# Cutting one V load of a decode attention kernel by partitions, with two small changes at head and tail

## The chip, the cores and the metric

The kernel runs on one core of a Trainium2 chip; the other cores are idle. The metric is the device time of the kernel in microseconds (us), as the median over runs. The kernel before takes 1254.60 us (1254.50 to 1254.62 in five runs), so differences of a few tenths of a us can be seen.

## The reference

One query token attends to 4,096 keys and values, for 8 x 32 = 256 heads of 128 elements, all in bf16:

```
q: (8, 32, 1, 128)   k, v: (8, 32, 4096, 128)
scores = einsum('bhqd,bhkd->bhqk', q, k) * 128 ** -0.5
attn   = softmax(scores)
out    = einsum('bhqk,bhkd->bhqd', attn, v)
```

K and V are 268 MB each and every byte is used once. The kernel is a stream of loads with some arithmetic beside it.

## The kernel before

The 256 heads are worked on in 32 tiles (NT) of 8 heads. A tile of K or of V is `[128 partitions, C = 256 positions, 128]` in bf16: 8 MB, one contiguous row of 64 KB for each partition. There are two K buffers and one V buffer. All loads are issued by SyncE, in program order; `cuts` says which loads are cut by position, and `("v", NT - 1)` is the last load of all.

```python
    cuts = {
        ("k", 0): [C // 4, C // 4, C // 2],
        ("k", NT - 4): [C // 2] * 2,
        # ... NT - 3, NT - 2, NT - 1 are cut as well
        ("v", NT - 1): [C // 2, C // 4, C // 8, C // 16, C // 32, LAST, LAST],
    }

    def load(kind, t):
        # ... choose pool and buffer
        c0 = 0
        for n in cuts.get((kind, t), [C]):
            nc.sync.dma_start(buf[:, c0 : c0 + n, :], src[t, :, c0 : c0 + n, :])
            c0 += n
            if kind == "k" and t == 0 and c0 == n:
                nc.sync.dma_start(q_all[:], q_n)
```

For each tile VectorE multiplies K by q and adds the two halves (in four quarters), TensorE sums the rest over the head dimension by matmuls with the identity, ScalarE makes the weights, and 64 matmuls apply them to V. At the end the sums are copied out of PSUM and combined:

```python
    def copy_of(t):
        comb = small.tile([P, CB, D], BF16, name="comb", tag="comb")
        av = avs.pop(t)[:].rearrange("p (m d) -> p m d", d=D)
        n = CB if t < NT - 1 else CB // 2
        nc.scalar.activation(out=comb[:, 0:n, :], in_=av[:, 0:n, :], func=ACT.Copy)
        if n < CB:
            nc.vector.tensor_copy(out=comb[:, n:CB, :], in_=av[:, n:CB, :])
        combs[t] = comb
```

## Time and profile before

| | before |
|---|---|
| median time | 1254.60 us |
| read from memory | 536.94 MB, 429 GB/s over the span |
| DMA engines busy | 99.3% (loads alone) |
| VectorE, TensorE, ScalarE busy | 77%, 44%, 27% |
| last landing mark of the last V load | 1248.64 us of a span of 1252.8 us |

The kernel is bound by its loads. The only idle DMA time is at the very end, where sixteen engines that begin level (the marks of the first load, explained below, lie within 0.4 us) do not end together. The lines of the page, the windows and the timeline that show this stand in the prediction below.

One view needs an explanation, because the argument rests on it. Every load of this kernel leaves sixteen *landing marks* in the trace. I read them as one for each DMA engine that took part: in 1,177 of the 1,252.8 us exactly sixteen packets of loads are under way (my count from the trace). The marks of one load, as a distance from its last one, show how far each engine is ahead. For the last load of the kernel before (my extract of the trace, us ahead of the last mark):

```
6.21 6.11 5.93 5.90 5.80 5.30 | 1.85 1.66 1.65 1.64 1.62 1.55 1.49 1.43 1.11 | 0
```

Six engines are early, nine are late, one is last. "Row" below means one packet of the trace, on one engine: 64 KB of a whole load (2.42 us in the median of 7,424), 32 KB of a half (1.22 us in the median of 1,152).

### The profile page before, as it was taken

The page shows a single profiled execution, that of the slowest core. Times are in us where ns is not written, and L with a number is a line of the kernel's source. Part 1 is how long each engine was busy: PE and PEld are TensorE (multiplying, and loading weights), DVE is VectorE, ACT ScalarE, POOL GpSimd, SP SyncE. Part 2 cuts the span into 40 slices and gives each one's busy share as a digit, 9 for nine tenths or more (in the row PEclk, how much of TensorE's full clock was granted, in tenths as well). Part 3 has the DMA queues.
Part 4 walks back from the last instruction along what each step waited for, and adds up shares of the span by engine and source line. Part 5 has one row for each costly group of instructions (what it writes and reads, how often), then busy time and mean ns, then how long its engine had stood idle before and what let it go on. Part 6 is the DMA issues. An engine that isn't in the chain of part 4 may idle for free.

```text
span 1252.8 us, 8134 instructions
## 1 busy us (share of the span) xinstructions
PE 554.0 (44%) x3299; PEld 202.6 (16%) x3299; DVE 967.6 (77%) x531; ACT 343.3 (27%) x625; POOL 6.0 (0%) x26
## 2 busy tenths in 40 slices
PE   2444543345534355333453334542445434545356
PEld 0111111111111111111111111111112111211112
DVE  7877887777977779777797777886778877977981
ACT  0333123331233321333213333123330333311333
POOL 1000000000000000000000000000000000000000
PEclk8667666667657767576765776666676766676777
DMA  9999999999999999999999999999999999999997
GB/s 404 435 436 432 434 435 433 434 432 434 435 434 436 434 429 429 431 432 433 434 434 436 430 436 436 436 434 435 432 427 427 437 433 432 434 420 431 430 439 311
DMA packets 11734, 537.53 MB, mean 429 GB/s; under 512 B 1840, under 2 KB 2096, under 8 KB 2352
## 3 DMA queue, kind: packets, MB, share of 16 engines
q1 hardware_dynamic: 11360, 536.94, 99.3%
q8 instruction: 26, 0.43, 0.1%
q10 hardware_dynamic: 336, 0.07, 0.0%
q14 instruction: 12, 0.10, 0.0%
HBM read 536.94 MB, written 0.07 MB: 429 GB/s over the span
## 4 chain that ended last, share of the span: by engine, by line
DMA 79%; PE 14%; DVE 6%; issue 0%; SPq 0%; another core or an unknown queue 0%; ACT 0%
DMA vt<-in_v_dram 78%; PE av L256 13%; DVE kt L175 3%; DVE kt L178 2%; PE ps L190 1%; DMA q_all<-in_q_dram 1%; DVE sc L202 0%; SPq L147 0%; DVE pmax L212 0%; DVE spread L214 0%; DVE nmax L219 0%; DVE comb L286 0%; ACT comb L284 0%; ACT stage L310 0%
## 5 line engine op out<-in xcount | busy, mean ns | idle before, releaser
L175 DVE TENSOR_TENSOR kt<-kt,qb 128x8192 bf16<-128x8192 bf16 x128 | 565.2, 4415 | 181.9 <-DMA kt<-in_k_dram 175.3
L190 PE MATMUL ps<-kt,ident 128*128 128x512 bf16 x1024 | 353.6, 508 | 572.1 <-DVE kt L178 572.1
L231 ACT ACTIVATE w<-sc,bias 128x256 bf16<-128x256 f32 x256 | 300.5, 1587 | 260.5 <-DVE bias L223 260.5
L178 DVE TENSOR_TENSOR kt<-kt 128x4096 bf16<-128x4096 bf16 x128 | 293.4, 2292 | 4.4
L190 PEld LDWEIGHTS <-ident 128*128 128x128 bf16 x1024 | 119.6, 119 | 775.5 <-issue 506.1
L256 PE MATMUL av<-vt,w 128*32 128x512 bf16 x2047 | 176.5, 513 | 90.0 <-DMA vt<-in_v_dram 90.0
L202 DVE TENSOR_REDUCE sc<-ps 128x64 f32<-128x512 f32 x128 | 87.8, 686 | 68.1 <-PE ps L190 68.1
L284 ACT ACTIVATE comb<-av 128x512 bf16<-128x512 f32 (+1 forms) x32 | 19.5, 609 | 413.1 <-PE av L256 413.1
L231 ACT ACTIVATION_READ_ACCUMULATOR w<-sc,bias 128x1 f32 x256 | 126.6, 495 | 0.0
L256 PEld LDWEIGHTS <-w 128*32 128x32 bf16 x2047 | 68.7, 125 | 207.1 <-DMA vt<-in_v_dram 107.8
L163 ACT ACTIVATE qg<-qh 8x128 bf16<-8x128 f32 x32 | 8.5, 266 | 165.9 <-PE qh L159 165.9
L310 ACT ACTIVATE stage<-op,rz 16x128 bf16<-16x128 f32 x16 | 5.9, 371 | 56.4 <-DVE rz L276 41.3
L301 PE MATMUL op<-comb,pick 128*16 128x128 bf16 x128 | 13.4, 230 | 12.8 <-ACT comb L284 12.4
L212 DVE TENSOR_REDUCE pmax<-sc 128x1 f32<-128x256 f32 x32 | 13.4, 420 | 1.1
L165 PE MATMUL qp<-qg,heads 8*128 8x128 bf16 x32 | 7.5, 235 | 12.7 <-ACT qg L163 12.7
L276 DVE RECIPROCAL rz<-zp 16x1 f32<-16x1 f32 x16 | 2.4, 149 | 13.9 <-PE zp L268 13.9
L159 PE MATMUL qh<-q_all,ident 128*8 128x128 bf16 x32 | 8.2, 256 | 8.3 <-DMA q_all<-in_q_dram 8.3
L167 ACT ACTIVATE qb<-qp 128x128 bf16<-128x128 f32 x32 | 8.9, 277 | 10.4 <-PE qp L165 10.4
L301 PEld LDWEIGHTS <-pick 128*16 128x16 bf16 x128 | 7.6, 91 | 21.0 <-issue 20.9
L214 DVE TENSOR_SCALAR spread<-same,pmax 128x32 f32<-128x32 f32 x32 | 7.7, 241 | 1.1
L223 DVE TENSOR_SCALAR bias<-own,nmax 128x8 f32<-128x8 f32 x32 | 7.4, 231 | 1.1
L219 DVE TRANSPOSE_TENSOR_REDUCE nmax<-spread 128x1 f32<-128x32 f32 x32 | 6.8, 211 | 1.1
(27 smaller groups left out, 20.1 us busy)
## 6 DMA issues: line engine op xcount, KB each, us to landing
kt<-in_k_dram SPq DMA_DIRECT2D x8, 4096.0 KB, 43.0
kt<-in_k_dram SPq DMA_DIRECT2D x4, 2048.0 KB, 23.3
vt<-in_v_dram SPq DMA_DIRECT2D x1, 4096.0 KB, 41.4
vt<-in_v_dram SPq DMA_DIRECT2D x1, 2048.0 KB, 45.9
vt<-in_v_dram SPq DMA_DIRECT2D x1, 1024.0 KB, 47.8
vt<-in_v_dram SPq DMA_DIRECT2D x1, 512.0 KB, 48.6
vt<-in_v_dram SPq DMA_DIRECT2D x31, 33.3
kt<-in_k_dram SPq DMA_DIRECT2D x27, 47.4
```

What stands on the lines that cost most here:

```text
L159: nc.tensor.matmul(qh[:], lhsT=ident[:, p0 : p0 + G], rhs=q_all[:, x, :], start=True, stop=True)
L163: nc.scalar.activation(out=qg[:], in_=qh[:], func=ACT.Copy)
L167: nc.scalar.activation(out=qb[:, 0, :], in_=qp[:], func=ACT.Copy)
L175: nc.vector.tensor_tensor(out=part, in0=part, in1=qb[:].to_broadcast([P, MC, D]), op=ALU.mult)
L178: nc.vector.tensor_tensor(out=part[:, :, 0 : D // 2], in0=part[:, :, 0 : D // 2], in1=part[:, :, D // 2 : D], op=ALU.add,)
L190: nc.tensor.matmul(ps[:], lhsT=ident[:], rhs=kt[:, u * UC : (u + 1) * UC, s * DS : (s + 1) * DS], start=(s == 0), stop=(s == n - 1),)
L202: nc.vector.tensor_reduce(out=scs[t][:, u * UC : (u + 1) * UC], in_=sums.pop((t, u))[:], axis=AX.X, op=ALU.add)
L212: nc.vector.tensor_reduce(out=pmax[:], in_=sc[:], axis=AX.X, op=ALU.max)
L231: nc.scalar.activation(out=w[:, :, g], in_=sc[:], func=ACT.Exp, bias=bias[:, g : g + 1], scale=scale, accum_out=esum[:, t % R, g : g + 1],)
L256: nc.tensor.matmul(avs[t][j * AG : (j + 1) * AG, :], lhsT=w[:, c0 : c0 + CB, :], rhs=vt[:, c0 : c0 + CB, :], start=(i < TG), stop=(j not i ...
L284: nc.scalar.activation(out=comb[:, 0:n, :], in_=av[:, 0:n, :], func=ACT.Copy)
L301: nc.tensor.matmul(ops[n][:], lhsT=pick[:, m, r, :], rhs=comb[:, m, :], start=(r == 0 and m == 0), stop=(r == R - 1 and m == CB - 1),)
```

## The change

Its intent can be read from the arithmetic. In one V load in the middle of the kernel, twelve engines carry one row less and four carry three more, which would even out the end. Beside that it starts with a longer first K piece, drops the cut of one late K load, puts three of the last tile's matmuls into other groups of sums, and makes the last copy in one piece.

```diff
-        ("k", 0): [C // 4, C // 4, C // 2],
-        ("k", NT - 4): [C // 2] * 2,
+        ("k", 0): [C // 2] * 2,
...
+        ("v", NT // 2): [C // 2] * 2,
...
-            nc.sync.dma_start(buf[:, c0 : c0 + n, :], src[t, :, c0 : c0 + n, :])
+            parts = [(0, P)]
+            if (kind, t, c0) == ("v", NT // 2, 0):
+                parts = [(0, P - 16)] + [(p, p + 4) for p in range(P - 16, P, 4)]
+            for lo, hi in parts:
+                nc.sync.dma_start(buf[lo:hi, c0 : c0 + n, :], src[t, lo:hi, c0 : c0 + n, :])
...
-            0 if t == NT - 1 and C // 2 <= c0 < 3 * C // 4 else c0 // CB % TG
+            0 if t == NT - 1 and C // 2 <= c0 < C // 2 + 3 * C // 16 else c0 // CB % TG
...
-        n = CB if t < NT - 1 else CB // 2
-        nc.scalar.activation(out=comb[:, 0:n, :], in_=av[:, 0:n, :], func=ACT.Copy)
-        if n < CB:
-            nc.vector.tensor_copy(out=comb[:, n:CB, :], in_=av[:, n:CB, :])
+        nc.scalar.activation(out=comb[:], in_=av, func=ACT.Copy)
```

## The prediction

> **What bounds the kernel now.** I read the page first: the slices over time, the DMA queues, the chain that ended last. Then I read the windows of the last 20 us, the chain and timeline of the tail, and the landing marks of single loads.
>
> ```profile
> DMA  9999999999999999999999999999999999999997
> GB/s 404 435 436 432 434 435 433 434 432 434 435 434 436 434 429 429 431 432 433 434 434 436 430 436 436 436 434 435 432 427 427 437 433 432 434 420 431 430 439 311
> ...
> q1 hardware_dynamic: 11360, 536.94, 99.3%
> q8 instruction: 26, 0.43, 0.1%
> ...
> q14 instruction: 12, 0.10, 0.0%
> ...
> DMA 79%; PE 14%; DVE 6%; issue 0%; SPq 0%; another core or an unknown queue 0%; ACT 0%
> ```
>
> The DMA row is 9 in every slice but the last, so transfers bound this kernel. VectorE (77% busy) and TensorE (44%) work in their shadow. The bytes, 536.94 MB, are fixed by the inputs. The change alters no byte, so it can win only at the head, at the tail, or in how evenly the sixteen DMA engines end. The windows of the tail show that last one (columns: stretch, length, busy time per engine, granted clock, DMA share, GB/s):
>
> ```profile
> 1230.00:1240.00 10.00, 4.95 (x64) 2.32 (x60) 0.00 (x0) 8.51 (x17) 0.21 (x1) 0.84 0.96 406
> 1240.00:1246.00 6.00, 4.69 (x37) 2.30 (x30) 0.15 (x1) 0.00 (x0) 0.00 (x0) 0.82 0.75 306
> 1246.00:1249.00 3.00, 2.94 (x26) 1.24 (x24) 0.00 (x0) 0.23 (x1) 0.00 (x0) 1.00 0.20 68
> ```
>
> The DMA share falls to 0.75 and then 0.20 while V is still arriving: some engines have finished and wait for the others. The landing marks give the amounts. Every load leaves sixteen, one per engine. For the last load they lie 6.2, 6.1, 5.9, 5.9, 5.8, 5.3 us (six engines), then 1.85 to 1.1 us (nine engines) before the last one, which alone sets 1248.64. The mean lead is 3.1 us: all that perfect balance could win. The lead grows steadily. The first load's marks lie within 0.4 us; at the V load with index 16, landing near 683.8 us, the six lead by 2.9 to 3.3 us.
>
> The cause can be read from the packets. A 64 KB row takes 2.42 us on its engine, back to back. The 26 instruction packets of 16 KB each hit one engine: beside one, a row took about 2.89 us and the next began about 1.07 us later, so a fetch costs its engine some 1.55 us. They come round about every 390 us, to eight different engines in turn. 26 x 1.55 = 40 us, plus the twelve 8 KB fetches at about 0.7 us (a stretched row and a 0.31 us gap), is 48.7 us; the sum of the sixteen leads is 49.2. So the skew is fetch time, and it falls on ten engines while six stay free.
>
> After the DMA ends, this remains (timeline):
>
> ```profile
> 1248.68 0.38 PE L296 MATMUL op<-vt,w_last 128*16 128x128 bf16 x4
> 1248.77 0.38 ACT L284 ACTIVATE comb<-av 128x256 bf16<-128x256 f32 x1 [10.26 <-PE av L256]
> 1249.19 0.42 DVE L286 CAST comb<-av 128x256 bf16<-128x256 f32 x1 [6.60 <-ACT comb L284]
> 1249.21 0.27 PE L301 MATMUL op<-comb,pick 128*16 128x128 bf16 x2
> 1249.67 0.27 PE L301 MATMUL op<-comb,pick 128*16 128x128 bf16 x2 [0.19 <-DVE comb L286]
> 1249.97 0.36 ACT L310 ACTIVATE stage<-op,rz 16x128 bf16<-16x128 f32 x1 [0.82 <-PE op L301]
> ```
>
> The two half copies do not run side by side: VectorE's waits for ScalarE's.
>
> [...]
>
> **The change part by part.**
> 1. The V load with index 16 comes in halves. In the first half, every engine carries 7 rows instead of 8[...]. A 32 KB row takes 1.21 us in the trace (1213 to 1221 ns). So twelve engines gain 1.21 us, and four lose 3 x 1.21 = 3.63 us. If the four are among the six free ones, they fall back by 4.84 us against the rest, from a lead of 5.3 to 6.2 us to one of 0.5 to 1.4 us. The last mark is then still one of the twelve's, 1.21 us earlier. At index 16 itself the lead is about 3 us, so that load lands 0.6 us later at most: 3.63 less 3. Its successor K load (19.3 us of transfer) hides that. **-1.2 us.** The size of the shift, 4.84 us, fits the lead so well that I take it for chosen after seeing which engines are ahead.
> 2. First K load: halves for quarters. The first quarter landed at 8.1 us; a half lands some 4.9 us later (2 MB at 430 GB/s). VectorE's first tile, done near 41 us, ends near 46, and K load 2 is issued then instead of at 40.98. V load 0 keeps the engines occupied until 61.6 us, so nothing runs dry. VectorE needs about 30 us of each 38.7 us period and catches up. **0.**
> 3. K load NT-4 whole: VectorE starts that tile 9.7 us later, but it has about 8 us of slack per tile, and the next three K loads are still cut. **0.**[...]
> 4. Group of the last tile's matmuls: the same 31 matmuls after the half, and each piece is awaited from DMA. **0.**
> 5. Last copy whole: removed are 0.38 + 0.42 us plus the handover, 1248.77 to 1249.61, 0.84 us. Added is one 128x512 ScalarE copy, mean 0.617 us. But two of the four result matmuls ran beside the VectorE half, and now all four follow; four took 0.39 to 0.59 us elsewhere, against 0.27. 0.84 - 0.62 - 0.12 = 0.1. **-0.1 us.**
> 6. Five more load instructions on SyncE at 0.33 to 0.46 us each; SyncE idles for hundreds of us. **0.**
>
> Sum: 1254.57 - 1.2 - 0.1 = 1253.3.
>
> **The rivals.**
> [...]
> - *Wrong engines.* If engines 0 to 3 are among the fetching ten, they set the end: between 1.11 us behind which they start and the last one itself, 3.63 us more is +1.8 to +3.6, near 1257. Nothing in the trace numbers its engines, so I can't exclude this.
> - *Hidden anyway.* If TensorE paced the tail, a DMA that ends 1.2 us earlier would win less. The weights are done at 1238.1, the 32 matmuls on the first half at 1242.35, and the next piece lands at 1243.65: 1.3 us of slack, just enough. 1254.
>
> **Range and chances.** I give 1253.3 by the sum about 60%, a partial or no gain (1253.7 to 1254.6) 15%, wrong engines 10%[...]. I predict 1253.4, a little above the sum; range 1252.3 to 1259[...]. Two per cent is 25 us: no case wins that[...].
>
> **What the profile after would show.** Right: in the last load's landing marks the spread shrinks from 6.2 to about 2 us, the DMA share of the last windows stays higher, and the last V mark comes near 1247.4. The tail holds one ScalarE copy of about 0.6 us, then four result matmuls. The VectorE start at 14 instead of 9.6 us leaves no trace later.[...] Wrong engines: rows of 1.21 us, but a spread above 6 us at the end.[...]

Its sum came to 1253.3 us (1254.57 - 1.2 - 0.1). Part 1 rests on the deal of rows above; before the run it was an assumption. "Engines 0 to 3", here and in the expectations, is only a name for the four engines that a 4-partition load uses: the trace doesn't number engines. Cut are what no trace or run of this case shows, and one rival with its 15%: that the four rows of a small load hold each other up. Its 1267 to 1272 us rested on an estimate, four rows of 1.21 us one after the other, 4.84 us for each small load. That the 16 KB fetches hit eight engines in turn is read from the packets: the rows just behind them take 2.88 to 2.97 us, and their lengths recur with every eighth fetch, 388.6 us later (65.75, 454.31, 842.87 us).

## The result, and the profile after

The changed kernel takes 1273.37 us (1272.88 to 1275.88, five runs) against 1254.60. The ratio is 1.0154 (95% interval 1.014 to 1.0168). Ratios here are the mean time of one kernel's fast runs over that of the other's fast runs of the same rounds, so not quite the ratio of the medians that I quote. The loss is 18.8 us: within two per cent, but far outside the stated range, and on the wrong side.

The page of the changed kernel, the same rows as shown of before:

```profile
DMA  9999999999999999999999999999999999999996
GB/s 406 454 427 428 427 433 431 429 444 431 429 430 429 444 429 436 433 431 431 429 385 277 439 431 431 430 437 431 438 434 429 428 431 438 436 433 419 431 439 264
...
DMA 82%; PE 14%; DVE 3%; another core or an unknown queue 0%; issue 0%; SPq 0%; ACT 0%
```

The DMA row is as full as before, but the engines moved less in the same time: 385 and 277 GB/s in the two slices from about 636 to 699 us, where V load 16 runs. **Busy is not moving at full speed**, and only the GB/s row tells. Windows of ten us make it sharp. First the kernel before (columns as in the prediction; the last is GB/s):

```profile
660.00:670.00 10.00, 0.00 (x0) 0.10 (x1) 5.51 (x2) 7.05 (x14) 0.00 (x0) 0.50 0.97 419
670.00:680.00 10.00, 6.04 (x17) 2.05 (x17) 9.97 (x6) 0.90 (x3) 0.00 (x0) 0.67 0.98 421
680.00:690.00 10.00, 6.84 (x66) 2.31 (x64) 9.97 (x4) 0.00 (x0) 0.00 (x0) 0.54 1.06 460
```

Then the changed kernel:

```profile
650.00:660.00 10.00, 4.27 (x26) 1.74 (x22) 6.25 (x8) 2.70 (x6) 0.00 (x0) 0.91 1.00 428
660.00:670.00 10.00, 0.00 (x0) 0.10 (x1) 1.97 (x1) 7.25 (x14) 0.00 (x0) 0.50 1.00 226
670.00:680.00 10.00, 3.98 (x10) 1.26 (x10) 9.93 (x5) 0.90 (x3) 0.00 (x0) 0.57 1.03 251
680.00:690.00 10.00, 3.13 (x8) 0.89 (x7) 9.97 (x6) 0.00 (x0) 0.00 (x0) 0.77 0.98 201
690.00:700.00 10.00, 3.60 (x32) 1.39 (x33) 5.98 (x2) 0.00 (x0) 0.00 (x0) 0.50 1.03 416
```

For 30 us the rate is about half (226 GB/s on average against 433). That alone is 30 x (1 - 226/433) = 14.3 us of lost transfer. In the packets of the trace, the 32 KB rows of the 112-partition load took 2.3 to 2.5 us in the main (2.36 in the median of the first 112), on *all sixteen* engines, in place of 1.21 (of the 23 rows that began between 664 and 668 us, none took less than 2.3), the last 64 KB rows of the K load before it up to 5.0 in place of 2.42, and rows of the full second half beside the small loads took 2.4 to 2.9.

In the chain of waits of the changed kernel, V load 16 is seen as a wait of 42.67 us and a second one, in place of about 33 us for the V loads before it and 35.02 for the next (start, length, what; the unknown queue is the second half, which landed at 703.75):

```profile
651.67 42.67 DMA vt<-in_v_dram
694.55 3.60 PE av L261 x32
698.15 5.60 another core or an unknown queue
703.80 3.63 PE av L261 x32
707.44 35.02 DMA vt<-in_v_dram
```

The end differs too. The windows of its last us:

```profile
1250.00:1260.00 10.00, 5.53 (x67) 2.86 (x63) 0.00 (x0) 7.63 (x15) 0.21 (x1) 0.67 0.88 365
1260.00:1264.00 4.00, 3.20 (x25) 1.40 (x18) 0.16 (x1) 0.00 (x0) 0.00 (x0) 0.71 0.20 81
1264.00:1268.00 4.00, 3.35 (x29) 1.39 (x28) 0.00 (x0) 0.42 (x1) 0.00 (x0) 1.00 0.09 34
```

A DMA share of 0.125 would be two engines of sixteen. From about 1262 us no more than that are at work. The landing marks of the last load say the same (us ahead of the last, at 1267.45):

```
11.24 10.88 10.60 9.84 | 7.05 6.99 6.96 6.95 6.68 6.60 6.53 6.23 5.90 5.28 | 1.17 0
```

The early group of six has become four, the late group ten, and two engines end more than 5 us after everybody else. So there are two losses. The engine that was last before is not one of the two (the probe below shows it), so at the slowest it now has the mark at 5.28: 1262.17 against 1248.64, **13.5 us** later; this is what the slow stretch costs all. The two stragglers add **5.3 us**. The sum is 18.8.

The tail after the loads went as foreseen (timeline of the changed kernel):

```profile
1267.49 0.38 PE L298 MATMUL op<-vt,w_last 128*16 128x128 bf16 x4
1267.58 0.60 ACT L288 ACTIVATE comb<-av 128x512 bf16<-128x512 f32 x1 [9.95 <-PE av L261]
1268.23 0.38 PE L303 MATMUL op<-comb,pick 128*16 128x128 bf16 x4 [0.36 <-ACT comb L288]
1268.65 0.36 ACT L312 ACTIVATE stage<-op,rz 16x128 bf16<-16x128 f32 x1 [0.47 <-PE op L303]
```

From the start of the copy to the start of the stage write it takes 1.07 us, against 1.20 before.

### The profile page after: what moved, and what is told of

It is laid out like the page before. It is cut to its first block, busy times and chain, and to the rows that moved or that the text cites. A ratio compares the mean times of both kernels' runs of the same rounds, so it can differ in the third digit from the quotient of the medians.

```text
span 1271.3 us, 8138 instructions
## 1 busy us (share of the span) xinstructions
PE 550.3 (43%) x3299; PEld 201.1 (16%) x3299; DVE 967.4 (76%) x530; ACT 343.3 (27%) x625; POOL 6.0 (0%) x26
## 4 chain that ended last, share of the span: by engine, by line
DMA 82%; PE 14%; DVE 3%; another core or an unknown queue 0%; issue 0%; SPq 0%; ACT 0%
DMA vt<-in_v_dram 78%; PE av L261 13%; DMA kt<-in_k_dram 3%; DVE kt L180 2%; DVE kt L183 1%; DMA q_all<-in_q_dram 1%; PE ps L195 1%; SPq L152 0%; DVE sc L207 0%; ACT comb L288 0%; DVE pmax L217 0%; PE op L303 0%; ACT stage L312 0%; ACT qb L172 0%
## 5 line engine op out<-in xcount | busy, mean ns | idle before, releaser
L195 PE MATMUL ps<-kt,ident 128*128 128x512 bf16 x1024 | 348.9, 503 | 584.1 <-DVE kt L183 584.1
L288 ACT ACTIVATE comb<-av 128x512 bf16<-128x512 f32 x32 | 19.7, 616 | 420.3 <-PE av L261 420.3
L303 PE MATMUL op<-comb,pick 128*16 128x128 bf16 x128 | 13.0, 226 | 13.2 <-ACT comb L288 13.2
L164 PE MATMUL qh<-q_all,ident 128*8 128x128 bf16 x32 | 8.0, 250 | 13.2 <-DMA q_all<-in_q_dram 13.2
```

What stands on the lines that cost most here:

```text
L164: nc.tensor.matmul(qh[:], lhsT=ident[:, p0 : p0 + G], rhs=q_all[:, x, :], start=True, stop=True)
L195: nc.tensor.matmul(ps[:], lhsT=ident[:], rhs=kt[:, u * UC : (u + 1) * UC, s * DS : (s + 1) * DS], start=(s == 0), stop=(s == n - 1),)
L288: nc.scalar.activation(out=comb[:], in_=av, func=ACT.Copy)
L303: nc.tensor.matmul(ops[n][:], lhsT=pick[:, m, r, :], rhs=comb[:, m, :], start=(r == 0 and m == 0), stop=(r == R - 1 and m == CB - 1),)
```

## The experiments

Fourteen kernels ran, each beside runs of the kernel before on the same chip (its medians: 1254.53 to 1254.64). My theory after reading the result: which partitions a load covers decides, and one on fewer than 128 slows the rows of all engines; on top, the four engines of the small loads are not all early. The rivals: another part of the change costs; only the four small loads cost; only the number of engines or rows counts; the memory rows read count. The mechanism that I had in mind for the theory isn't shown by any run; the trace doesn't record which engine writes which partitions. The label `w_one_port` is a name and no finding.

### Which part of the change

`e1_rest` is the changed kernel with the first half of V load 16 as one load:

```diff
-            if (kind, t, c0) == ("v", NT // 2, 0):
-                parts = [(0, P - 16)] + [(p, p + 4) for p in range(P - 16, P, 4)]
```

> The changed kernel without the five-part first half of V load 16 (which now comes as two 128-partition halves); all other parts kept. Theory: the whole loss comes from the five-part load, so 1254.5 us (1254.2 to 1254.7), 0.1 below before because of the whole last copy. Rival: the later compute start (first K load in halves, 14 us instead of 9.6) or K load NT-4 as a whole costs something: over 1256 us.

Measured: 1254.49 us (1254.27 to 1254.84), ratio 0.9999 (0.9985 to 1.0013). The other parts are harmless; a gain of 0.1 us can't be told from chance.

`e2_split` is the kernel before plus the five-part half only (the two hunks of the diff on `cuts` for `NT // 2` and on `parts`).

> The kernel before plus only the five-part first half of V load 16. Theory: the loss stays whole, 1272.5 to 1274.5 us. Rival (other parts have a share): clearly below 1272 us.

Measured: 1272.92 us (1272.63 to 1273.17), ratio 1.0145. The five-part half has the whole loss.

### The 112-partition load, or the four small ones

`e3_112_16` (from `e2_split`):

```diff
-                parts = [(0, P - 16)] + [(p, p + 4) for p in range(P - 16, P, 4)]
+                parts = [(0, P - 16), (P - 16, P)]
```

> As e2_split, but the last 16 partitions come as one load on sixteen engines (one row each) and not as four loads on four engines. Theory that the partition set of a load decides[...]: the 112-partition rows stay at about 2.4 us in place of 1.21 (7 rows, +8.4 us)[...], and no engine carries more rows than another, so about 1266 us (1263 to 1268). Rival, that only the four 4-partition loads cost: 112-partition rows at 1.21 us, and 1254.6 to 1258.5 us.

A term of this sum is cut: +3.6 us for the 16-partition row, from an estimate of up to 4 x 1.21 = 4.84 us in place of 1.21. With it the sum is 1254.6 + 8.4 + 3.6 = 1266.6.

Measured: 1266.79 us (1266.39 to 1266.82), ratio 1.0096. Its windows from 660 to 690 us show 220, 243 and 293 GB/s:

```profile
670.00:680.00 10.00, 3.93 (x10) 1.25 (x10) 9.93 (x5) 0.90 (x3) 0.00 (x0) 0.57 1.00 243
680.00:690.00 10.00, 5.29 (x40) 1.84 (x40) 9.97 (x6) 0.00 (x0) 0.00 (x0) 0.83 0.95 293
```

With no 4-partition load at all, two thirds of the loss stay; the 112-partition load's rows are at 2.3 to 2.5 us as before. But a 16-partition load is still there, so this run doesn't isolate the 112-partition one. An estimate from its packets (the time of each row above 2.42 or 1.21 us, in order of start, summed and divided by sixteen engines): the 64 KB rows lost 1.4 us, the first 112 rows of 32 KB 6.9 and the later ones 3.7, together 12.0 of the 12.2 us. In the changed kernel the three are 1.3, 6.9 and 6.8 us. Loads overlap, so the border after 112 rows is rough. The marks at its end are again grouped as six, nine and one, with 6.6 us between first and last: no engine was put behind. But the 16-partition row took about 2.4 to 2.7 us, not the 4.84 that I had estimated, so the time was met for partly wrong reasons.

`e4_strided` (from `e2_split`) keeps the four engines, but each small load takes every fourth partition:

```diff
+                parts = [(0, P - 16, 1)] + [(P - 16 + i, P, 4) for i in range(4)]
...
+                nc.sync.dma_start(buf[lo:hi:by, c0 : c0 + n, :], src[t, lo:hi:by, c0 : c0 + n, :])
```

> As e2_split, but each of the four loads takes every fourth of the last 16 partitions (112+i, 116+i, 120+i, 124+i)[...]; engines and rows per engine unchanged. [...]the slow stretch of the 112-partition load stays (+8.4 less 1.2 us), that of the small loads shrinks, engines 0 to 3 still carry 3 rows more: 1262 to 1268 us.[...] If it is the mere use of four engines[...]: as e2_split, 1273 us.

The case that is cut here, 1255 to 1259 us, was that only the small loads on adjacent partitions cost. That every fourth partition leaves the deal to the engines as it is was an assumption.

Measured: 1270.15 us (1269.75 to 1270.43), ratio 1.0123: a miss, between the figures of the theory and of the last rival. Taking every fourth partition in place of adjacent ones gave back less than 3 of 18 us. In the stretch of the small loads all rows, of every engine, took about 2.4 us. So whether the partitions of a small load are adjacent is not the main measure of the loss.

### 64 partitions at a time

`e5_64_64` (from `e2_split`) has no small load, and was meant to deal its rows evenly to all sixteen engines:

```diff
-                parts = [(0, P - 16)] + [(p, p + 4) for p in range(P - 16, P, 4)]
+                parts = [(0, P // 2), (P // 2, P)]
```

> The kernel before, with the first half of V load 16 as two loads of 64 partitions each, on sixteen engines with four rows each: no engine carries more rows than another. [...]the rows take 2.42 us in place of 1.21 and the half 19.4 in place of 9.7 us: 1264.3 us (1262 to 1266). Rival (only the number of engines or rows matters[...]): 1254.6 us (1254.2 to 1255.2).

Measured: 1267.78 us (1267.20 to 1268.20), ratio 1.0104. Its windows:

```profile
660.00:670.00 10.00, 0.00 (x0) 0.10 (x1) 1.62 (x1) 7.14 (x14) 0.00 (x0) 0.50 1.00 213
670.00:680.00 10.00, 4.03 (x10) 1.30 (x10) 9.93 (x5) 0.91 (x3) 0.00 (x0) 0.50 1.02 227
```

The rival that only the number of engines or rows matters falls: in these windows the rate is 213 to 227 GB/s, in place of about 433. The 112-partition load ran at the same half rate (226 and 251 GB/s above). The loss is 13.2 us and not 9.7, above the range that I gave, because rows of the full loads around it were slowed as well: the K rows before it took up to 5.3 us while some engines had gone on to the 64-partition load. By the same sum over packets they lost 1.4 us, the first 128 rows of 32 KB 9.7, and the rows after those 1.7. That is 12.8 of the 13.2 us, so slower rows make up the loss, and hardly any of it is left for an uneven deal.

### Which engines are early

`e6_probe` leaves the bulk as it is and cuts only the last 128 KB load by partitions:

```diff
+            if (kind, t, c0) == ("v", NT - 1, C - LAST):
+                parts = [(0, 96), (96, 112), (112, 120), (120, 124), (124, 126), (126, 127), (127, 128)]
```

> The kernel before, with its last 128 KB load cut by partitions into 96, 16, 8, 4, 2, 1 and 1, so that the landing marks tell which engines are early[...]. Time 1254.6 to 1255.2 us. If all of engines 0 to 3 are ahead (what the prediction took), the four marks of the 4-partition load come 5 to 6 us before the last mark of the 96-partition load. If two of them are not (what the end of the changed kernel suggests, where two engines end 5 us after the rest), two of those marks come 0 to 2 us before it.

Measured: 1255.03 us (one run). The load of eight partitions left eight marks, 6.2, 5.9, 5.6, 5.1 and 2.1, 1.5, 1.3, 1.0 us ahead of the last engine's mark: four early engines, four late ones, and not the last. The load of four partitions left two marks 1.3 us after its issue (3.8 ahead: those engines were idle already), and two at 1.95 and 0.8 ahead. So two of its four engines are early. The other two are late: they fit the marks at 2.3 and 1.15 in the load before. With 3.63 us added to both, they would stay 2.3 - 1.15 = 1.15 us apart; the two stragglers of the changed kernel are 1.17 apart, as if its small loads had used the same four engines.

### At partitions 0 to 15 or at 112 to 127

Five kernels give wrong results. In all of them, three quarters of V load 16 come as one 128-partition load. The last quarter is set to zero, and only 16 of its partitions are loaded, by four loads of four partitions each. They differ in the partitions written and in the memory rows read.

```diff
+            if (kind, t, c0) == ("v", NT // 2, C - C // 4):
+                nc.gpsimd.memset(buf[:, c0:C, :], 0.0)
+                for lo, hi, by in [(i, 16, 4) for i in range(4)]:        # w_home
+                # [(P - 16 + i, P, 4) for i in range(4)]                    w_away
+                # [(p, p + 4, 1) for p in range(P - 16, P, 4)]              w_one_port
+                    nc.sync.dma_start(buf[lo:hi:by, c0:C, :], src[t, lo:hi:by, c0:C, :])
```

"Home" is my name for partitions 0 to 15 and "away" for 112 to 127. The trace doesn't record partitions by engine.

> Wrong result on purpose: of the last quarter of V load 16 only partitions 0 to 15 are loaded (the rest is set to zero), by four loads of every fourth partition[...]. 8 rows of 0.61 us are missing on every engine, so 1249.7 us if those four rows on engines 0 to 3 cost nothing (they are ahead), 1250.3 to 1252.2 us if one of the engines 0 to 3 is among the late ones. Rows of the small loads 0.61 us, rows of others undisturbed.

> As w_home, but the four loads take every fourth of partitions 112 to 127[...]. [...]later than w_home by 1 to 4 us. Rival ([...]only which engines carry rows): the same time as w_home within 0.3 us.

> As w_away, but each of the four loads takes four adjacent partitions (112 to 115 and so on), as in the changed kernel[...]. [...]rows of the small loads take 2.4 to 3 us for 16 KB[...], or at least more than in w_away; later than w_away by 1 to 6 us. Rival (only which engines carry rows): the same as w_home and w_away.

The 2.4 to 3 us here were an estimate, from four rows of 0.61 us one after the other.

The two crossed ones take the data of one set for the partitions of the other:

```diff
-  w_home:  src[t, lo:hi:by, c0:C, :]
+  x_dst_home:  src[t, P - 16 + lo : P : by, c0:C, :]
-  w_away:  src[t, lo:hi:by, c0:C, :]
+  x_dst_away:  src[t, lo - (P - 16) : 16 : by, c0:C, :]
```

> Wrong result on purpose. As w_home (small loads land in partitions 0 to 15), but their data are read from where w_away read them in memory (rows of partitions 112 to 127). If the slowdown of all sixteen engines in w_away comes from the partitions written: undisturbed rows and 1250.9 us, as w_home. If it comes from the memory rows read: 1255.7 us, as w_away.

> Wrong result on purpose. As w_away (small loads land in partitions 112 to 127), but their data are read from the rows of partitions 0 to 15. If the partitions written decide: 1255.7 us with K rows of 3.5 to 4.4 us beside the small loads, as w_away. If the memory rows read decide: 1250.9 us.

| kernel | partitions written | memory rows of | time, us |
|---|---|---|---|
| w_home | 0 to 15, every fourth | 0 to 15 | 1250.91 (1250.64 to 1251.24) |
| x_dst_home | 0 to 15, every fourth | 112 to 127 | 1250.76 (1250.66 to 1250.85) |
| w_away | 112 to 127, every fourth | 112 to 127 | 1255.69 (1255.58 to 1255.77) |
| x_dst_away | 112 to 127, every fourth | 0 to 15 | 1255.80 (1255.61 to 1255.94) |
| w_one_port | 112 to 127, adjacent | 112 to 127 | 1254.61 (1254.24 to 1254.66) |

The window in which the small loads ran, in w_home:

```profile
675.00:685.00 10.00, 7.30 (x73) 2.68 (x73) 9.93 (x5) 0.54 (x2) 0.00 (x0) 0.83 1.01 434
```

in x_dst_home:

```profile
675.00:685.00 10.00, 7.32 (x62) 2.69 (x65) 9.93 (x5) 0.54 (x2) 0.00 (x0) 0.60 1.00 433
```

in w_away:

```profile
675.00:685.00 10.00, 6.63 (x58) 2.37 (x57) 9.93 (x5) 0.54 (x2) 0.00 (x0) 0.83 1.06 280
```

and in x_dst_away:

```profile
675.00:685.00 10.00, 6.28 (x57) 2.29 (x56) 9.93 (x5) 0.28 (x2) 0.00 (x0) 0.83 0.99 249
```

**The partitions written decide, the rows read don't.** Four loads of the same bytes are free of cost to others at one place (434 and 433 GB/s; small rows of 16 KB at 0.61 us, K rows at 2.42) and nearly halve the rate of *all* engines at another (280 and 249 GB/s; small rows about 1.25 us, K rows on the other engines 3.5 to 4.75). The 1250.9 us of w_home are also the probe's answer over again: 1254.6 less 8 missing rows of 0.61 us is 1249.7, and the late engine that is 1.15 us from the end carries 4 x 0.61 = 2.43 us, 1.3 us more than its lead: 1251.0. w_away came 4.8 us after w_home where I had given 1 to 4: I had expected only some engines to slow down.

w_one_port is a miss for my theory: four adjacent partitions were no worse than every fourth one, even 1.1 us better. With 32 KB rows behind a 112-partition load it was the other way round: e2_split, adjacent, was 2.8 us slower than e4_strided. So adjacency has no fixed sign here. The small rows of w_one_port took 1.1 to 1.2 us in the main.

Why the place decides, no run shows. A slowness of partitions 112 to 127 themselves isn't excluded by these five; but the first of the 64-partition loads and the 112-partition load write partitions 0 to 63 and 0 to 111, and were slow too (213 and 226 GB/s).

### Is the skew made of instruction fetches?

`f_fewer` and `f_fewer2` spare 128 and 320 TensorE instructions: in 16 or 40 of the 128 score quarters VectorE adds once more, and four of the eight matmuls and weight loads fall away.

```diff
+            if c0 == Q and 4 <= t < 20:              # f_fewer2: c0 in (Q, 3 * Q) and 4 <= t < 24
+                nc.vector.tensor_tensor(
+                    out=part[:, :, 0 : D // 4], in0=part[:, :, 0 : D // 4],
+                    in1=part[:, :, D // 4 : D // 2], op=ALU.add,
+                )
...
-        n = D // 2 // DS
+        n = D // 2 // DS // (2 if u == 1 and 4 <= t < 20 else 1)      # likewise
```

> The kernel before with 128 fewer TensorE instructions (in sixteen of the 128 score quarters VectorE adds once more, 32 elements wide, and four matmuls are saved). If the engine that ends last does so because it carries a fourth instruction fetch at 1231.9 us, that fetch moves past the last V row and the end comes with the next engine, 1.1 to 1.5 us earlier: 1253.0 to 1253.6 us. Rival (the lag has another cause than fetches): 1254.6 us or, with the added VectorE work, more.

> As f_fewer, with 320 TensorE instructions fewer than before (forty score quarters with one more VectorE addition each). In f_fewer the twenty-fifth fetch only moved from 1231.9 to 1242.6 us, still ahead of the last V rows, and put its engine 1.3 us behind the rest again. Here it should move past 1248 us, and the end comes with the other engines: 1253.0 to 1253.7 us. If the added VectorE work (40 x 1.2 us) is not hidden, or if the lag has another cause: 1254.5 us or more.

f_fewer measured 1254.77 us (1254.31 to 1255.09), ratio 1.0001: no gain, a miss, at the time of the rival. But its marks answer the question. Its last fetch moved to 1242.8 us (the second expectation has 1242.6). In the V pieces that land before it, the last two engines are 0.14 to 0.16 us apart; in those after it 1.34 us. One fetch makes the last engine last. The first fetch of the kernel before shows the same: the marks of the load that ended at 61.6 us lie within 0.34 us, and after the fetch at 65.8 us those of the next have one engine 1.3 to 1.6 us behind all others. In f_fewer2 only 24 fetches are left, the last at 1232.7, and the last two engines end 0.15 us apart.

f_fewer2 measured 1253.54 us (1253.37 to 1254.28) beside 1254.53 (1254.38 to 1254.94), ratio 0.9993 with an interval of 0.9981 to 1.0006, so not clear of chance, though all five runs lie below the nine beside them. `f_best` adds the whole last copy.

> As f_fewer2 with the one part of the change that the prediction counted as a gain and that is free of the loads: the last copy whole on ScalarE. Theory: 1 us from the fetch that moved past the end, and 0.1 us from the copy: 1253.4 us (1253.0 to 1253.8), and below every run of before. Rival (f_fewer2's gain was chance): 1254.3 us or more.

Measured: 1254.28 us (1253.24 to 1254.70) beside 1254.56, ratio 0.9994 (0.9981 to 1.0008). This is a miss: two runs came at 1253.2 to 1253.4 and three at 1254.3 to 1254.7. I claim no better version. The chain of waits of the profiled run (1254.33 us) says why the gain stops:

```profile
1230.03 9.39 ACT w L236 x16
1239.42 0.43 ACT comb L288
...
1240.48 3.41 PE av L261 x29
...
1243.92 4.88 PE av L261 x28
...
1248.83 0.61 ACT comb L288
```

No load stands in it any more. The last V mark comes about 1.0 us earlier (1247.62), and the last tile's weights on ScalarE and the matmuls behind them are the end. In the kernel before they are hidden behind the loads by 1.3 us, the wait of TensorE for the V piece at 1243.65. In f_best the weights also start 1.4 us later than before (1230.03 against 1228.58), so part of what is missing may be the price of the added work itself; no run separates this. Evening out the engines can win about 1.3 us at most, where I had taken 3.1 us for the limit and 1.2 us for the change.

## Why the prediction was wrong

**What bounds the kernel: right.** Loads, with a skew at the end made by instruction fetches; f_fewer and f_fewer2 show that one fetch more or less sets the last engine. One sum was loose. The delays against the freest engine are what should match the fetch time, 16 x 6.21 - 49.2 = 50.2 us, and not the leads, 49.2; that both lie near 48.7 is chance.

**Step 1, "twelve engines gain 1.21 us, and four lose 3 x 1.21 = 3.63 us": wrong, and the step that failed.** I took 1.21 us, the row time of 128-partition loads, for the rows of every load. The rows of the 112-partition load take 2.3 to 2.5 us in the main on all engines, and the rows of the full loads beside it and beside the small loads slow down in like measure. This costs 13.5 us, where the step had a gain of 1.2. I had not asked at all what a 112-partition load does; e3_112_16 shows that two thirds of the loss need no 4-partition load, and by the estimate there some 8 of the 18.8 us were lost at the 112-partition rows and the K rows before them.

**"If the four are among the six free ones": wrong for two of them.** The probe finds two of the four late, one of them the second last of all. I reasoned that the size of the shift fitted the lead too well for chance; that was an argument about the author and not about the trace. It costs 5.3 us more: a lead of 1.11 us against 6.4 us of extra time relative to the rest (the step had 4.84; the rows were slow).

**"That load lands 0.6 us later at most": wrong.** Its last mark is at 703.75 us in place of about 684.

**Steps 2 to 6: right.** e1_rest is within 0.15 us of before. VectorE starts its first product at 14.41 us, as foretold, and it leaves no trace later. The whole copy saves 0.13 us of the tail (1.20 to 1.07; predicted 0.1).

**The rivals.** The one (four rows of a small load hold each other up) had the right direction and nearly the right time (1267 to 1272), but by luck: I let only the four engines of the small loads lose, while all sixteen lose, and w_one_port and e4_strided show that adjacent partitions are not the main measure (every fourth one gave back 2.8 us of 18 in one pair and lost 1.1 us in the other). *Wrong engines* is true as well; I had treated the two as alternatives, and they add up. *Hidden anyway*: the 1.3 us of slack that I read in the tail were gone in f_best.

**Range and chances: the weighing failed.** Nothing in the trace spoke against the rival, yet I gave it 15% and left it outside the range, because I trusted the change to have been kept for its gain. That no case wins two per cent came true; the loss is 1.5%.

**What stays open.** Why four loads of four partitions slow all engines at partitions 112 to 127 and none at 0 to 15; which partitions each engine writes, which the trace doesn't record; and why adjacent partitions were 1.1 us better than strided ones in w_one_port and 2.8 us worse in e2_split.

## What to carry to other kernels

In a kernel bound by loads, keep every large load at 128 partitions and cut it along the free dimension: here a 64- or 112-partition load, or four small ones at partitions 112 to 127, took the rate of all sixteen DMA engines from about 433 to between 188 and 313 GB/s over ten us, also for the full loads beside it. Read the GB/s row beside the DMA busy row, since busy engines at half speed look full (DMA share 1.00 at 226 GB/s). Before moving work between engines, find out which ones are early by a tiny load at the end (its landing marks tell), and how much slack the next bound leaves: here 1.3 us.
